# Attention and feed-forward in one planned kernel: products of probabilities and values share the score tiles' PSUM and are tied to a score pair

## The chip, the cores and the metric

The kernel runs on one core of a Trainium2 chip. The metric is the device time of one launch in microseconds (us). A measurement of this kernel can tell two versions apart from about 0.3% on.

## The reference

Block-sparse attention over 4 batches, 8 heads, 768 positions and 64 values per head, and then a feed-forward layer over the 3072 rows that it gives:

```
scores = scale * np.matmul(q, k.transpose(0, 1, 3, 2))
...
scores = np.where(mask, scores, -1000000000.0)
scores = scores - np.max(scores, axis=-1, keepdims=True)
attn = np.exp(scores)
attn = attn / (np.sum(attn, axis=-1, keepdims=True) + 1e-09)
return np.matmul(attn, v).astype(np.float32)
...
x = np.ascontiguousarray(attn_out.transpose(0, 2, 1, 3)).reshape(B * S, H * D)
h = x @ w_in
g = np.maximum(h, 0.0) + alpha * np.minimum(h, 0.0)
return (g @ w_out).astype(np.float32)
```

The mask lets each block of 32 positions see its neighbours, the first and last block and three drawn ones. Here `w_in` is 512x2048 and `w_out` 2048x512.

## The kernel before

**The work.** Everything is cut into chunks of 256 query rows (two tiles of 128), 12 chunks in all. A chunk has 4 units, one for each pair of heads; a unit `u` has two score pairs, one for each head. 32-bit values are split into a high and a low 16-bit part, so each product is taken three times (high by high, high by low, low by high).

**A score pair** is one step of the plan (`emit_s`, L603 to L619). It fills two PSUM tiles `sp` of 128x768 for two row tiles. Its first four matmuls (L611) use TensorE's whole 128x128 array. Its last four (L617) use halves of 64 rows, two matmuls at a time. VectorE then reads each tile (`emit_bias`, L627: scale, mask, row minimum `nm`), which I call the bias below. ScalarE takes the exponential (`emit_exp`, L634). The reciprocal of the row sum (`dn`, `rs`) and the split into `ph` high (`times`, L390 to L394) and low (`rest`, L398 to L401) follow on the engines that the plan chose, and a DMA transposes `ph` into `pt`.

**The products of a unit** (`emit_av`, L664 to L680) multiply `pt` by the split values: 36 matmuls that use halves of 64 columns, two heads side by side. The result `av` (128x256) goes to `x`: ScalarE writes the high part (`emit_x_hi`, L685), then VectorE the low part (`emit_x_lo`, L690). In the kernel before, `av` is a tile of the same pool as the score tiles, which has two buffers (`ps_s`, tag `s`). A score pair needs both.

**The feed-forward work** of a chunk is 8 groups `h` (`emit_up`, 24 matmuls, L1052) and 8 groups `o` (`emit_down`, 12 matmuls, L1094), which run between the pairs of the next chunk. VectorE makes `g` from `h` (L1062, L1063), ScalarE and GpSimd split it into `gh` and `gl`.

**The start.** For the first 125 us or so the kernel also turns the 64-bit weights into 32-bit ones and splits them (`wi`, `wo`; L858 to L870 on VectorE, L863 on ScalarE, L390 to L394, L955 and L960), and finds scales (`gsc`, `am1`).

**What sets the order.** `Plan.run` is a list scheduler that runs while the program is built. Each operation has a priority, the engines that it may run on with an assumed cost for each, the operations that it needs, and the buffers that it takes and frees. The order in which the scheduler starts the operations is the order in which their instructions are written, and each engine carries its own out in that order. The semaphores are put in afterwards by the framework, from the tiles that the written instructions read and write; the scheduler doesn't see them.

Of the kernel before, what the change touches and what calls it, by code (L numbers as in the profile page):

```python
# [8 lines left out]
F32 = mybir.dt.float32  # L9
# [18 lines left out]
MOE_LAG = 10.973  # L28
EARLY = 15.72
MOE_BOOST = 1.244  # L30
V_WA = -11.421
W_WA = 0.818
V_WB = 2.562
W_WB = 0.788
LDP = 47.514
PL_V = -45.149
P_V = 2.094
# [10 lines left out]
PREF = {"PE": 1.0, "DVE": 1.928, "ACT": 1.347, "POOL": 1.033, "SP": 1.0}  # L48
PREF0 = {"PE": 1.0, "DVE": 2.5, "ACT": 1.0, "POOL": 0.8, "SP": 1.0}
SLOW = 1.12  # L50
UNTIL = 130.0
Q_PE = 1
# [8 lines left out]
class Op:  # L61
    def __init__(self, n, prio, alts, fn, deps, alloc, use, dma):
        self.n, self.prio, self.alts, self.fn, self.dma = n, prio, alts, fn, dma
        self.deps = [d for d in deps if d is not None]
        self.alloc, self.use = alloc, use
        self.start = self.done = None
        self.eng = None


class Plan:  # L70
# [14 lines left out]
    def op(self, prio, alts, fn, deps=(), alloc=(), use=(), dma=None):  # L85
        o = Op(len(self.ops), prio, alts, fn, deps, list(alloc), list(use), dma)
        for b in o.alloc + o.use:
            b.users.append(o)
        self.ops.append(o)
        return o  # L90
# [12 lines left out]
    def run(self):  # L103
# [19 lines left out]
        busy = dict.fromkeys(self.ENGINES, 0.0)  # L123

# [28 lines left out]
        while left:  # L153
            progress = True
            while progress:
                progress = False
                ready.sort(key=lambda o: (o.prio, o.n))
                load = dict.fromkeys(self.ENGINES, 0.0)
                taken = []
                for o in ready:  # L160
# [60 lines left out]
def attn_moe(ctx: ExitStack, tc: tile.TileContext, q, k, v, sampled, w_in, w_out, alpha, out):  # L221
# [19 lines left out]
    plan = Plan(dict(bufs, s=2, h=2, o=2, ld=LD))  # L241
# [108 lines left out]
    def mask_cols_pe():  # L350
        mk["c"] = ps_s.tile([P, S], F32, tag="s", name="mk")
# [3 lines left out]
    def mask_rows_pe(t):  # L355
        mk[t] = ps_s.tile([P, S], F32, tag="s", name="mkr")
# [7 lines left out]
    mb = plan.buf("s")  # L364
# [3 lines left out]
    for t in range(NT):  # L368
        mb = plan.buf("s")
# [231 lines left out]
    def emit_s(n):  # L601
# [6 lines left out]
        for i in range(2):  # L608
            T["sp", n + i] = ps_s.tile([P, S], F32, tag="s", name="sp")
# [54 lines left out]
    def emit_av(u):  # L664
# [4 lines left out]
        av = T["av", u] = ps_s.tile([P, S], F32, tag="s", name="av")  # L669
# [109 lines left out]
    def attend(n):  # L779
# [23 lines left out]
    def values(u):  # L803
# [3 lines left out]
        ab = plan.buf("s")  # L807
        if hp == 0:
# [435 lines left out]
```

## Time and profile before

| | |
|---|---|
| Median of 3 runs | 834.72 us (833.66 to 836.19) |
| The profiled execution | 835.07 us, span 833.4 us |
| TensorE (PE) busy | 786.3 us, 94% of the span |
| VectorE (DVE) busy | 664.8 us, 80% |
| ScalarE (ACT) busy | 483.9 us, 58% |
| GpSimd (POOL) busy | 576.0 us, 69% |
| DMA queue q1 | 72.0% of 16 engines' span |

The busy share of TensorE is a mean over two stages: a start of some 126 us in which it has gaps, and the rest, in which it hardly stops. Which of the two a change touches decides what it is worth. A stretch of work that the profile gives as the time from one start to the next is what TensorE really spends on it; the single matmuls' own durations overlap.

### The profile page before, as it was taken

How to read it: one execution, taken by the hardware profiler on the slowest of the kernel's cores; microseconds unless marked ns; L12 is line 12 of the kernel's file. 1: busy time of each engine (PE TensorE's matmuls, PEld its weight loads, DVE VectorE, ACT ScalarE, POOL GpSimd, SP SyncE). 2: the span in 40 equal slices, each digit the busy share in tenths (PEclk: the TensorE clock that was granted, in tenths of full speed). 3: DMA queues.
4: the chain of work that ended last, by engine and by line, in shares of the span. 5: the costliest groups of instructions: out<-in, count | busy, mean ns of one | idle time of the engine just before them, and what ended most of it. 6: DMA issues, size and time to landing. Idle time of an engine off the chain costs nothing. (4 is left out here: it accounts for less than half of the span.)

```text
span 833.4 us, 16815 instructions
## 1 busy us (share of the span) xinstructions
PE 786.3 (94%) x6303; PEld 497.7 (60%) x6303; DVE 664.8 (80%) x1336; ACT 483.9 (58%) x898; POOL 576.0 (69%) x460
## 2 busy tenths in 40 slices
PE   4868669999999999999999999999999999999997
PEld 2423336666666666566665666666666675566764
DVE  5999889879789978788889797888799797676222
ACT  6988966765646455565566373756565564563111
POOL 5398777768768768578758777677878686666221
PEclk9799879999999999999999999999999999999999
DMA  9999784876878776878978758869898565754200
GB/s 336 322 288 227 180 180 98 189 165 148 192 164 193 147 171 116 206 118 200 199 165 174 152 122 169 192 141 203 168 196 147 135 150 117 156 111 107 59 7 25
DMA packets 386449, 136.13 MB, mean 163 GB/s; under 512 B 350628, under 2 KB 379328, under 8 KB 386368
## 3 DMA queue, kind: packets, MB, share of 16 engines
q1 hardware_dynamic: 386304, 135.04, 72.0%
q8 instruction: 49, 0.80, 0.4%
q14 instruction: 32, 0.26, 0.1%
q0 software_dynamic: 64, 0.02, 0.0%
HBM read 35.67 MB, written 6.29 MB: 50 GB/s over the span
## 5 line engine op out<-in xcount | busy, mean ns | idle before, releaser
L1052 PE MATMUL h<-x,wi 128*128 128x256 f16 x2304 | 267.9, 274 | 0.0
L634 ACT ACTIVATE e<-e,nm 128x768 f32<-128x768 f32 x192 | 178.7, 931 | 144.9 <-DVE nm L627 137.0
L1052 PEld LDWEIGHTS <-wi 128*128 128x128 f16 x2304 | 221.0, 98 | 49.3 <-issue 17.3
L1094 PE MATMUL o<-wo,gh 128*128 128x512 f16 x768 | 229.1, 380 | 0.0
L627 DVE CUSTOM_DVE_ANT_0 e<-sp,bias,cs 128x768 f32<-128x768 f32 x192 | 188.8, 1009 | 41.8 <-PE sp L617 41.3
L394 POOL TENSOR_SCALAR ph<-e,rs 128x768 f16<-128x768 f32 x95 | 97.9, 1031 | 144.5 <-PE sp L617 33.5
L401 POOL TENSOR_TENSOR ph<-e,ph 128x768 f16<-128x768 f32 x100 | 188.2, 1882 | 8.3
L1073 POOL TENSOR_TENSOR gl<-g,gh 128x512 f16<-128x512 f32 x96 | 125.3, 1307 | 57.4 <-ACT gh L1068 36.7
L1094 PE MATMUL o<-wo,gl 128*128 128x512 f16 x384 | 145.6, 379 | 0.6 <-POOL gl L1073 0.6
L398 DVE SCALAR_TENSOR_TENSOR ph<-e,rs,ph 128x768 f16<-128x768 f32 x92 | 135.6, 1474 | 4.3 <-ACT ph L390 2.8
L1068 ACT CAST gh<-g 128x512 f16<-128x512 f32 x96 | 59.2, 616 | 127.5 <-DVE g L1063 122.7
L1094 PEld LDWEIGHTS <-gh 128*128 128x128 f16 x768 | 68.8, 98 | 86.7 <-issue 12.8
L400 POOL TENSOR_SCALAR e<-e,rs 128x768 f32<-128x768 f32 x100 | 112.2, 1122 | 10.7 <-ACT ph L390 7.8
L674 PE MATMUL av<-pt,v 128*64 128x256 f16 x1728 | 105.4, 277 | 5.4 <-DVE nm L627 5.2
L1062 DVE SCALAR_TENSOR_TENSOR g<-h,am 128x512 f32<-128x512 f32 x96 | 65.7, 684 | 52.2 <-PE h L1052 52.0
L674 PEld LDWEIGHTS <-v 128*64 128x64 f16 x1728 | 92.1, 111 | 22.4 <-issue 15.2
L390 ACT ACTIVATE ph<-e,rs 128x768 f16<-128x768 f32 x75 | 69.4, 930 | 22.7 <-DVE rs L645 18.7
L1063 DVE SCALAR_TENSOR_TENSOR g<-h,gsc,g 128x512 f32<-128x512 f32 x96 | 72.1, 751 | 3.4
L1094 PEld LDWEIGHTS <-gl 128*128 128x128 f16 x384 | 37.5, 98 | 46.3 <-POOL gl L1073 1.1
L611 PEld LDWEIGHTS <-qt 128*128 128x128 f16 x384 | 37.6, 99 | 35.3 <-issue 13.2
L611 PE MATMUL sp<-kt,qt 128*128 128x512 f16 x192 | 48.2, 334 | 5.8 <-DVE x L690 4.1
L611 PE MATMUL sp<-ks,qt 128*128 128x512 f16 x192 | 48.3, 334 | 1.3 <-DVE nm L627 1.3
(147 smaller groups left out, 763.0 us busy)
## 6 DMA issues: line engine op xcount, KB each, us to landing
wo<-in_moe_w_in_dram SPq DMA_DIRECT2D x16, 512.0 KB, 6.3
raw<-in_moe_w_out_dram SPq DMA_DIRECT2D x16, 512.0 KB, 8.6
kf<-in_k_dram SPq DMA_DIRECT2D x16, 384.0 KB, 3.9
qf<-in_q_dram SPq DMA_DIRECT2D x12, 512.0 KB, 4.9
vf<-in_v_dram SPq DMA_DIRECT2D x16, 384.0 KB, 5.1
out_dram<-ob SPq DMA_DIRECT2D x24, 256.0 KB, 2.5
ks<-kt SPq DMA_DIRECT2D x30, 192.0 KB, 4.3
pt<-ph SPq DMA_TRANSPOSE x192, 3.4
```

Source lines behind the costliest of these rows:

```text
L394: nc.gpsimd.tensor_scalar(dst, src, scale, 1.0, ALU.mult, ALU.mult)
L398: nc.vector.scalar_tensor_tensor(dst, src, scale, hi, ALU.mult, ALU.subtract)
L400: nc.gpsimd.tensor_scalar(tmp, src, scale, 1.0, ALU.mult, ALU.mult)
L401: nc.gpsimd.tensor_tensor(dst, tmp, hi, ALU.subtract)
L611: nc.tensor.matmul(T["sp", n + i][:, a:z], T["qt", u][:, h, i, :], (ks, kt)[i][:, h, a:z], start=True, stop=False)
L627: nc.vector.tensor_tensor_reduce(T["e", n], T["sp", n], bias[:, t0 + j % w, :], scale=T["cs", c][:, hp : hp + 1], scalar=3.0e38, op0=ALU.a ...
L634: nc.scalar.activation(T["e", n], T["e", n], AF.Exp, bias=T["nm", n], scale=-1.0, accum_out=T["su", n])
L674: nc.tensor.matmul(av[h * D : (h + 1) * D, : n * P], v2[:, h, t, vv, :], T["pt", u, h][:, pl * NT + t, :], start=(m == 0), stop=(m == len( ...
L1052: nc.tensor.matmul(ph[:, i, :], win(w, f, ct), x[:, ct, :], start=(m == 0), stop=(m == len(terms) - 1))
L1063: nc.vector.scalar_tensor_tensor(g, ph, gs_[:, j : j + 1], g, ALU.mult, ALU.add)
L1073: nc.gpsimd.tensor_tensor(T["gl", c, j], T["g", c, j], T["gh", c, j], ALU.subtract)
L1094: nc.tensor.matmul(T["o", c][t], g[:, i, t * P : (t + 1) * P], wout(w, f), start=(i == 0 and m == 0 and j in first_j), stop=(i == 1 and m ...
```

## The change

The two score tiles become two fixed tiles of 128x1024, `sp[0]` and `sp[1]`. A score pair uses columns 0 to 767 of both, which its matmuls write in two parts, 0 to 511 and 512 to 767. The products of unit `u` go to columns 768 to 1023 of `sp[u % 2]`, right behind the second part. In the plan the products no longer take a score buffer (`s0` and `s1` are the pair's alone); they need `x` of unit `u - 2` to be done. Each TensorE operation has a mode, the array's division that it starts and ends with: 0 is the whole array, 1 halves of rows, 2 halves of columns. A change of division costs the plan `SWITCH` = 0.095, and while the array stands at 1, products are preferred by `JOIN` = 5.497. The products' own priority is later by `P_AV` = 6.123. Fifteen other numbers of the plan move a little, and the pair's and the products' own assumed costs.

```diff
-MOE_LAG = 10.973
+MOE_LAG = 10.963
...
-P_V = 2.094
+P_V = 2.751
...
+SWITCH = 0.095
+JOIN = 5.497
+P_AV = 6.123
...
-            return s * (sum(c) if isinstance(c, tuple) else c)
+            c = s * (sum(c) if isinstance(c, tuple) else c)
+            return c + SWITCH if e == "PE" and o.mode[0] != tiling else c
...
-                ready.sort(key=lambda o: (o.prio, o.n))
+                ready.sort(key=lambda o: (o.prio - JOIN if o.mode[0] == 2 and tiling == 1 else o.prio, o.n))
...
-    ps_s = ctx.enter_context(tc.tile_pool(name="ps_s", bufs=2, space=PSUM))
+    ps_s = ctx.enter_context(tc.tile_pool(name="ps_s", bufs=1, space=PSUM))
...
+    sp = [ps_s.tile([P, 1024], F32, tag=f"s{i}", name=f"sp{i}") for i in range(2)]
...
-            T["sp", n + i] = ps_s.tile([P, S], F32, tag="s", name="sp")
+            T["sp", n + i] = sp[i][:, :S]
...
-        av = T["av", u] = ps_s.tile([P, S], F32, tag="s", name="av")
+        av = T["av", u] = sp[u % 2][:, S:]
...
-            sbuf[n], sbuf[n + 1] = plan.buf("s"), plan.buf("s")
-            o_s[n] = o_s[n + 1] = plan.op(n, {"PE": 1.17}, lambda: emit_s(n), [o_qt[u], o_av.get(steps[max(n - 3, 0)][0] - 2)] + o_kt[b, hp] + o_ks[b, hp],
-                                          [sbuf[n], sbuf[n + 1]], [qtbuf[u], kbuf[b, hp], ksbuf[b, hp]])
+            sbuf[n], sbuf[n + 1] = plan.buf("s0"), plan.buf("s1")
+            o_s[n] = o_s[n + 1] = plan.op(n, {"PE": 1.07}, lambda: emit_s(n), [o_qt[u], o_av.get(steps[max(n - 3, 0)][0] - 2)] + o_kt[b, hp] + o_ks[b, hp],
+                                          [sbuf[n], sbuf[n + 1]], [qtbuf[u], kbuf[b, hp], ksbuf[b, hp]], mode=(0, 1))
...
-        o = o_av[u] = plan.op(p - 2, {"PE": 0.3 + 1.88 * f}, lambda: emit_av(u), last + [o_v2[b, hp]],
-                    [ab, xbuf[c]], [ptbuf[u, 0], ptbuf[u, 1], vbuf[b, hp]])
+        o = o_av[u] = plan.op(p - 2 + P_AV, {"PE": 0.05 + 1.92 * f}, lambda: emit_av(u), last + [o_v2[b, hp], o_x.get(u - 2)],
+                    [xbuf[c]], [ptbuf[u, 0], ptbuf[u, 1], vbuf[b, hp]], mode=(2, 2))
```

Eight lines are added ahead of the functions in question, so their lines move on by 9: the pair's are L620 and L626 after, the bias L636, the products L683, the high and low part of `x` L694 and L699, `h` L1060 and `o` L1102.

Three places of the two programs follow, with what each instruction waits for. A wait names the engine whose count it waits for; `DMAHW` are DMA transposes and loads.

First TensorE at the products of unit 28, the first of chunk 7. Before:

```order
L617 MATMUL sp_6974<-ks_5911,qt_6511 128x256
L1094 LDWEIGHTS gh_6916 [waits Activation_49]
...
L674 LDWEIGHTS v2_5207 [waits DMAHW1_49,DMAHW0_49]
L674 MATMUL av_7020<-pt_6776,v2_5207 64x256 [waits DVE_49]
...
L1052 LDWEIGHTS wi_88
...
L611 LDWEIGHTS qt_6511
L611 MATMUL sp_7107<-ks_5911,qt_6511 128x512 [waits DVE_49]
```

and after:

```order
L626 MATMUL sp1_74<-ks_5696,qt_6323 128x256
L683 LDWEIGHTS v2_5057 [waits DMAHW1_49]
L683 MATMUL sp0_73<-pt_6521,v2_5057 64x256 [waits DMAHW0_49]
...
L1102 LDWEIGHTS gh_6693 [waits Activation_49]
...
L620 LDWEIGHTS qt_6323
L620 MATMUL sp0_73<-ks_5696,qt_6323 128x512 [waits DVE_49]
```

Before, a group `o` stands between the pair and the products, and a group `h` between the products and the next pair; after, the products stand right behind the pair, and one group `o` is all that lies between them and the next pair, which waits for VectorE.

Second, VectorE at the same unit. Before:

```order
L627 ISA e_7008,nm_7009<-sp_6971,bias_110,cs_6117 128x768 [waits PE_49,Pool_49]
L398 SCALAR_TENSOR_TENSOR ph_7006<-e_6925,rs_6983,ph_7006 128x768 [waits DMAHW5_49,Pool_49]
L627 ISA e_7057,nm_7058<-sp_6974,bias_110,cs_6117 128x768 [waits PE_49]
...
L455 SCALAR_TENSOR_TENSOR qn_6810<-qf_6706,sq_6782,qn_6810 128x8x64
L690 SCALAR_TENSOR_TENSOR x_7019<-av_7020,x_7019 128x256 [waits Activation_49]
```

and after:

```order
L1071 SCALAR_TENSOR_TENSOR g_6754<-h_6706,gsc_121,g_6754 128x512 [waits DVE_49]
L636 ISA e_6798,nm_6799<-sp0_73,bias_112,cs_5854 128x768 [waits PE_49,Pool_49]
L407 SCALAR_TENSOR_TENSOR ph_6757<-e_6697,rs_6752,ph_6757 128x768 [waits DMAHW3_49,Pool_49]
L636 ISA e_6818,nm_6819<-sp1_74,bias_112,cs_5854 128x768
L699 SCALAR_TENSOR_TENSOR x_6759<-sp0_73,x_6759 128x256 [waits Activation_49]
```

The first bias waits for TensorE in both. Before, the count that it waits for is the one that the pair's last matmul on that tile sets; after, it is the one that the last of the 36 matmuls of the products sets, because both touch `sp0`. Of the 192 biases 173 wait for the pair and none for products before; after, 113 wait for the pair and 31 for products. The next pair's first matmul waits for the last row shown (`x`) in both programs.

Third, VectorE at the products of unit 23, the last of chunk 5. Before:

```order
L627 ISA e_5829,nm_5830<-sp_5731,bias_110,cs_4992 128x768 [waits DVE_49]
L627 ISA e_5834,nm_5835<-sp_5734,bias_110,cs_4992 128x768
...
L392 TENSOR_SCALAR ph_5905<-e_5834,rs_5898 128x768 [waits DMAHW6_49,DVE_49]
L690 SCALAR_TENSOR_TENSOR x_5118<-av_5839,x_5118 128x256 [waits Activation_49]
L398 SCALAR_TENSOR_TENSOR v2_5900<-vf_4637,sv_4918,v2_5900 128x12x64 [waits Pool_49]
```

and after, where the products lie in the second tile of the pair:

```order
L636 ISA e_5657,nm_5658<-sp0_73,bias_112,cs_4731 128x768 [waits DVE_49]
L636 ISA e_5701,nm_5702<-sp1_74,bias_112,cs_4731 128x768 [waits PE_49]
L407 SCALAR_TENSOR_TENSOR kn_5655<-kf_5566,ks_5648,kn_5655 128x12x64 [waits DMAHW3_49,DMAHW5_49,DMAHW2_49,Pool_49]
L650 TENSOR_SCALAR dn_5736<-su_5704 128x1 [waits Activation_49]
L654 RECIPROCAL rs_5741<-dn_5736 128x1 [waits DVE_49]
L407 SCALAR_TENSOR_TENSOR v2_5734<-vf_4390,sv_4904,v2_5734 128x12x64 [waits Pool_49]
L699 SCALAR_TENSOR_TENSOR x_4998<-sp1_74,x_4998 128x256 [waits Activation_49]
```

Before, neither bias waits for products, and `x` comes ahead of the values' split. After, the second bias waits for the products' last matmul; the splits of keys (`kn`) and values (`v2`) for the next batch and the low part of `x` stand behind it, and the pair after one group `h` waits for that `x`.

More of the change, by code (lines that the diff above doesn't have):

```diff
@@ L27 @@
 SIZES0 = [2, 2, 2]
-MOE_LAG = 10.973
+MOE_LAG = 10.963
 EARLY = 15.72
[L30 to L36, printed above, removed]
-P_V = 2.094
+MOE_BOOST = 1.237
+V_WA = -11.367
+W_WA = 0.771
+V_WB = 1.288
+W_WB = 0.74
+LDP = 49.245
+PL_V = -45.648
+P_V = 2.751
 PL = "gv"
@@ L47 @@
 LEADL = 2
-PREF = {"PE": 1.0, "DVE": 1.928, "ACT": 1.347, "POOL": 1.033, "SP": 1.0}
-PREF0 = {"PE": 1.0, "DVE": 2.5, "ACT": 1.0, "POOL": 0.8, "SP": 1.0}
+PREF = {"PE": 1.0, "DVE": 1.944, "ACT": 1.355, "POOL": 1.016, "SP": 1.0}
+PREF0 = {"PE": 1.0, "DVE": 2.183, "ACT": 0.98, "POOL": 0.948, "SP": 1.0}
 SLOW = 1.12
 UNTIL = 130.0
+SWITCH = 0.095
+JOIN = 5.497
+P_AV = 6.123
 Q_PE = 1
@@ L83, in buf, with op @@
         return Buf(pools)
-    def op(self, prio, alts, fn, deps=(), alloc=(), use=(), dma=None):
-        o = Op(len(self.ops), prio, alts, fn, deps, list(alloc), list(use), dma)
+    def op(self, prio, alts, fn, deps=(), alloc=(), use=(), dma=None, mode=(0, 0)):
+        o = Op(len(self.ops), prio, alts, fn, deps, list(alloc), list(use), dma, mode)
         for b in o.alloc + o.use:
@@ L123, in run @@
         busy = dict.fromkeys(self.ENGINES, 0.0)
+        tiling = 0
         def finish(o):
@@ L175, in run @@
                             port["from"], port["to"] = now + self.SLACK[best] * o.alts[best][0], now + c
+                    if best == "PE":
+                        tiling = o.mode[1]
                     o.eng, o.start = best, now
@@ L350, in mask_cols_pe @@
     def mask_cols_pe():
-        mk["c"] = ps_s.tile([P, S], F32, tag="s", name="mk")
+        mk["c"] = sp[1][:, :S]
         for a, z in ((0, 512), (512, S)):
@@ L355, in mask_rows_pe @@
     def mask_rows_pe(t):
-        mk[t] = ps_s.tile([P, S], F32, tag="s", name="mkr")
+        mk[t] = sp[t % 2][:, :S]
         for a, z in ((0, 512), (512, S)):
@@ L363, in attn_moe @@
     o_tab.deps.append(plan.op(-20, {"POOL": 9.0}, lambda: None))
-    mb = plan.buf("s")
+    mb = plan.buf("s1")
     o_mc = plan.op(-20, {"PE": 0.9}, mask_cols_pe, [o_tab], [mb], [pbuf])
@@ L368, in attn_moe @@
     for t in range(NT):
-        mb = plan.buf("s")
+        mb = plan.buf(f"s{t % 2}")
         o = plan.op(-12 + 5 * t, {"PE": 0.9}, lambda t=t: mask_rows_pe(t), [o_tc], [mb], [pbuf, pbuf2])
@@ L806, in values @@
         f = w / 2
-        ab = plan.buf("s")
         if hp == 0:
@@ L811, in values @@
         last = [x for n in range(first[u], first[u + 1]) for x in o_pt[n]]
-        o = o_av[u] = plan.op(p - 2, {"PE": 0.3 + 1.88 * f}, lambda: emit_av(u), last + [o_v2[b, hp]],
-                    [ab, xbuf[c]], [ptbuf[u, 0], ptbuf[u, 1], vbuf[b, hp]])
-        o = plan.op(p - 4, {"ACT": 0.1 + 0.2 * f}, lambda: emit_x_hi(u), [o], [], [ab, xbuf[c]])
-        o_x[u] = plan.op(p - 4, {"DVE": 0.1 + 0.25 * f}, lambda: emit_x_lo(u), [o], [], [ab, xbuf[c]])
+        o = o_av[u] = plan.op(p - 2 + P_AV, {"PE": 0.05 + 1.92 * f}, lambda: emit_av(u), last + [o_v2[b, hp], o_x.get(u - 2)],
+                    [xbuf[c]], [ptbuf[u, 0], ptbuf[u, 1], vbuf[b, hp]], mode=(2, 2))
+        o = plan.op(p - 4, {"ACT": 0.1 + 0.2 * f}, lambda: emit_x_hi(u), [o], [], [xbuf[c]])
+        o_x[u] = plan.op(p - 4, {"DVE": 0.1 + 0.25 * f}, lambda: emit_x_lo(u), [o], [], [xbuf[c]])
     al = cpool.tile([P, NF], F32, name="al")
```

6 lines of the change are left out of this document (3 added, 3 removed).

## The prediction

> **What bounds the kernel now.** I read the page's busy shares and slices first, then the busy time of each engine by stretches, the chain that ended last, and the list of who waited for whom.
>
> ```profile
> span 833.4 us, 16815 instructions
> PE 786.3 (94%) x6303; PEld 497.7 (60%) x6303; DVE 664.8 (80%) x1336; ACT 483.9 (58%) x898; POOL 576.0 (69%) x460
> PE   4868669999999999999999999999999999999997
> PEclk9799879999999999999999999999999999999999
> ```
>
> ```profile
> 20.00:126.00 106.00, 76.28 (x522) 39.04 (x522) 97.36 (x223) 90.21 (x142) 76.11 (x62) 0.85 0.96 240
> 200.00:300.00 100.00, 99.74 (x816) 64.41 (x814) 85.07 (x165) 54.42 (x108) 74.06 (x57) 1.00 0.81 174
> 400.00:500.00 100.00, 99.73 (x821) 64.66 (x820) 86.35 (x170) 56.65 (x111) 75.49 (x59) 1.00 0.75 160
> ```
>
> There are two stages. Up to 126 us VectorE is the busy one (third figure, 97.36 of 106 us) and TensorE has gaps. From then on TensorE works 99.7 of every 100 us at full clock, VectorE 85. So in the second stage any TensorE time that falls away is won in full, and any new TensorE wait is lost in full; VectorE has 15 us in 100 to give. What TensorE spends on each group is in the chain (start, time to the next piece, work):
>
> ```profile
> 692.05 2.62 PE h L1052 x24
> 694.67 2.09 PE av L674 x36
> 696.76 2.70 PE o L1094 x12
> 699.45 0.65 PE sp L611 x4
> 700.10 0.43 PE sp L617 x4
> 704.31 2.73 PE h L1052 x24
> 769.18 2.59 PE o L1094 x12
> ```
>
> A group `h` takes 2.62 us behind `o` and 2.73 behind the pair's halved matmuls (L617); a group `o` takes 2.59 behind `h` and 2.70 behind products. So a change of the array's division costs 0.11 us, in both kinds. Who waits:
>
> ```profile
> PE av L674 <- DVE nm L627: 5.2, 2, 4.5
> PE sp L611 <- DVE x L690: 4.1, 4, 2.6
> DVE e L627 <- PE sp L617: 40.9, 28, 2.9
> ```
>
> TensorE's waits at the touched work are few and mostly in the start. VectorE, on the other hand, comes to a bias too early 28 times and waits 1.5 us on average for the pair. These are the places where holding the bias longer bites at once.
>
> **The change, part by part.**
>
> *Fewer changes of division.* In the order, 34 of the 48 product groups stand right behind a pair after the change, none before. Rows to columns is then one change where there were two (back to whole, and on to columns). 34 x 0.11 = 3.7 us less, 32 of the 34 in the second stage where nothing hides it. No row shows a change straight from halved rows to halved columns. Bounds: 0 saved if it costs as much as two, 7.5 if it costs nothing; I take one change, as both kinds in the rows cost the same. By the Trainium skill (TensorEngine Tiling (Array Packing), Key Properties) a switch of the tiling mode drains TensorE, while moving to another tile of the same mode doesn't; by that rule the direct switch is one drain, and this term stays; no run here shows it yet.
>
> *The bias waits for the products.* This is the price. Products and scores lie in one tile, and after the change 31 biases are held until the last of the 36 matmuls is done, 2.09 us later than the pair. VectorE works in order, so everything behind the bias is held too, and the next pair needs both biases and the low part of `x`. Whether TensorE feels it is a comparison of two sums, between the products' end and the next TensorE instruction that waits for VectorE: TensorE's groups against VectorE's rows. The timeline (start, duration, engine) gives VectorE's steps and the gaps between the engines:
>
> ```profile
> 506.71 0.41 DVE L690 SCALAR_TENSOR_TENSOR x<-av,x 128x256 f16<-128x256 f32 x1
> 507.17 0.48 PE L611 MATMUL sp<-kt,qt 128*128 128x512 f16 x2 [0.50 <-DVE x L690]
> 508.48 1.01 DVE L627 CUSTOM_DVE_ANT_0 e<-sp,bias,cs 128x768 f32<-128x768 f32 x1
> 509.41 1.01 DVE L627 CUSTOM_DVE_ANT_0 e<-sp,bias,cs 128x768 f32<-128x768 f32 x1
> 510.35 0.08 DVE L627 DVE_READ_ACCUMULATOR2_ANT nm<- 128x1 f32 x1
> 519.20 0.60 PE L1094 MATMUL o<-wo,gh 128*128 128x512 f16 x2
> 519.41 1.02 DVE L627 CUSTOM_DVE_ANT_0 e<-sp,bias,cs 128x768 f32<-128x768 f32 x1 [2.64 <-PE sp L617]
> ```
>
> and the groups of 200 to 700 us (count, busy us, mean ns) the other durations:
>
> ```profile
> L398 DVE SCALAR_TENSOR_TENSOR ph<-e,rs,ph 128x768 f16<-128x768 f32 x66 | 102.2, 1549 | 1.5 <-ACT ph L390 1.4
> L392 DVE TENSOR_SCALAR ph<-e,rs 128x768 f16<-128x768 f32 x20 | 19.9, 997 | 0.7
> L455 DVE SCALAR_TENSOR_TENSOR qn<-qf,sq,qn 128x512 f16<-128x512 f32 x16 | 17.7, 1108 | 0.0
> L398 DVE SCALAR_TENSOR_TENSOR v<-vf,sv,v 128x768 f16<-128x768 f32 x11 | 14.8, 1347 | 3.3 <-ACT v L390 2.4 <-POOL v L394 0.8
> L398 DVE SCALAR_TENSOR_TENSOR kn<-kf,ks,kn 128x768 f16<-128x768 f32 x9 | 10.6, 1176 | 0.0
> ```
>
> One bias to what follows takes 0.94 us (508.48 to 509.41 to 510.35), some 0.07 less than its own duration, since the next one starts before it has ended; I take the same 0.07 off the other means, and 0.08 for `dn` or `rs`. From the start of TensorE's next group to a bias held by TensorE are 0.21 us (519.20 to 519.41), from the end of `x` to the pair 0.05 (506.71 + 0.41 to 507.17).
>
> - Unit 28, shown in the change, and units 24, 36 and 40 with the same rows: 0.21 + bias 0.94 + low `ph` 1.48 + bias 0.94 + `x` 0.41 + 0.05 = 4.03 us on VectorE, against one group `o` of 2.70: short by 1.3, four times, 5.3 us.
> - Units 23 and 35: 0.21 + bias 0.94 + `kn` 1.11 + `dn`, `rs` 0.16 + `v` 1.28 + `x` 0.41 + 0.05 = 4.16, against `h` 2.73 and half of the pair's first part 0.33: short by 1.1, twice, 2.2 us.
> - Unit 12: 0.21 + bias 0.94 + `rs` 0.08 + `qn` 1.04 + bias 0.94 + `dn` 0.08 + high `ph` 0.93 + `x` 0.41 + 0.05 = 4.68, against `h` 2.73: short by 1.9.
> - Units 4, 6, 8 and 11, summed in the same way over stretches of 3 to 15 us, are short by 1.4, 0.6, 1.0 and 0.3: 3.3 us.
>
> Together 12.7 us. The same comparison over the order of before finds no stretch that is short, and indeed its TensorE hardly waits there. Below: 0, if VectorE is late at these biases anyway. Above: with the full durations instead of the steps, and 1.09 for a bias with its read-out, the same sum is 31 us after and 9 before, so 22 more. I take 12.7, since the smaller steps are the ones that fit the 99.7 of 100.
>
> The Trainium skill has the rule that speaks against the change (PSUM — Partial Sum Buffer, PSUM bank collisions raise a hardware error): two engines must not touch one bank (512 of these columns) and 32-partition quadrant at once, even at other columns of it, so their accesses have to be put in order. Score columns 512 to 767 and the products at 768 to 1023 are one bank by that. By this rule the held bias is no accident of this order, and 845 us stands; without it the scores could be read while the products run, which would give 831. Before, products and scores had tiles of their own, so its trace can't show this.
>
> *The score buffers.* Products take no score tile any more. That ends the wait of 4.5 us and its like, which lie in the start, where VectorE is what the end hangs on. In the second stage a pair still waits for `x` of the last products on its tile.
>
> *The start.* TensorE has the same number of instructions ahead of its first group `h` in both programs, and the same work behind it. VectorE gets more to do ahead of the scale `gsc`: two L865, one high part of `wi` and four of `wo`, one copy of `qt`, one `rs`, and five `dn` fewer.
>
> First the pair and the first `h` of before, then those groups up to 126 us:
>
> ```profile
> 125.49 0.55 PE L611 MATMUL sp<-kt,qt 128*128 128x512 f16 x2 [2.61 <-DVE x L690]
> 126.72 0.61 PE L1052 MATMUL h<-x,wi 128*128 128x256 f16 x2
> ```
>
> ```profile
> L865 DVE SCALAR_TENSOR_TENSOR wo<-raw,wo 128x512 int32<-128x512 int32 x3 | 2.7, 898 | 0.1
> L392 DVE TENSOR_SCALAR wi<-wi,ssc 128x512 f16<-128x512 f32 x2 | 1.5, 762 | 0.0
> L641 DVE TENSOR_SCALAR dn<-su 128x1 f32<-128x1 f32 x14 | 2.0, 143 | 1.8 <-ACT e L634 1.8
> L556 ACT COPY qt<-qp 128x512 f16<-128x512 f16 x4 | 2.6, 700 | 0.0
> ```
>
> 2 x 0.90 + 5 x 0.76 + 0.70 (the copy by ScalarE's row, VectorE has none) + 0.15 - 5 x 0.14 = 5.8 us. VectorE was idle for 106 - 97.4 = 8.6 us there, and ScalarE gets less to do. Bounds: -4 (the buffer waits were on the path) to +5.8 (nothing absorbs it). I take +1.5, between them and nearer to a busy VectorE.
>
> *Covered.* The other numbers of the plan only move work about; the tile's address itself costs nothing, as the matmuls' shapes stay.
>
> **The sum.** The profiled execution took 835.07 us, 0.35 above the median of the runs. 835.1 - 3.7 + 12.7 + 1.5 = 845.6; less 0.35, about 845.
>
> **Rivals.**
>
> 1. *VectorE has room, faster.* If VectorE comes to the held biases later than the products end, because ScalarE or GpSimd hold it ahead of them, term two is 0 and 835.1 - 3.7 = 831. For it: VectorE has 15 us in 100 free, and two rows of `g` stand ahead of the bias at unit 28. Against it: the 40.9 us that it waits for pairs already. It decides as soon as TensorE's new waits stay under 3.7 us together, that is under 0.35 at each of the eleven places. Chance 0.18.
> 2. *It cancels.* If VectorE is half late at the held biases, the places are short by some 4 us together; with no change in the start 835.1 - 3.7 + 4 - 0.35 = 835. Chance 0.09.
> 3. *No change of division is saved*, since rows to columns passes through the whole array: 845 + 3.7 = 849. Against it: nothing in the rows needs it. Chance 0.13.
> 4. *The start is late by all of the 5.8 us*, and delayed biases reach ScalarE's and GpSimd's parts too: 850 or more. Chance 0.13.
>
> **How the numbers follow.** The forecast (840 to 848) has 0.47, and 845 is its middle. 0.3%, 2.5 us, is about what a measurement of this kernel can tell from no change. Slower by more: 0.47 + 0.13 + 0.13 = 0.73; within: 0.09; faster: 0.18. The range goes from 832, which leaves out about half of rival 1, to 857, which leaves out the end of rival 4 and with it the 22 us. Among the slower cases alone it is 840 to 857.
>
> **What would show it.** In the profile after: chain rows in which `h` or `o` behind a pair's products and nothing else is 0.11 longer, and products right behind a pair still at 2.09 (one change; 2.20 for rival 3). A wait of the bias for products (L636 <- PE, L683) of many us on VectorE. TensorE waits of 1 to 2 us on `x` (L699) and on `nm` (L636) at units 12, 23, 24, 28, 35, 36 and 40, some 13 us in all after the first `h`; busy TensorE in 200 to 700 us down from 99.7 to about 98. The first `h`, at 126.7 before, between 124 and 132 us. The prediction is wrong if VectorE waits for products but TensorE doesn't wait for VectorE.

## The result: 846.7 us, 1.45% slower, and the profile after

| | before | after |
|---|---|---|
| Median, 4 runs each on one chip | 834.83 us (833.66 to 836.19) | 846.74 us (846.01 to 848.27) |
| Ratio, 95% interval | | 1.0145 (1.0123 to 1.0166) |
| The profiled execution, its span | 835.07 us, 833.4 us | 848.27 us, 846.1 us |
| First `h` after the span's start | 126.7 us | 132.3 us |
| TensorE idle behind it, gaps over 0.1 us | 2.8 us in 7 | 13.1 us in 20 |

The forecast was 845. From the page of the changed kernel:

```profile
span 846.1 us, 16778 instructions
PE 787.1 (93%) x6303; PEld 501.7 (59%) x6303; DVE 649.7 (77%) x1345; ACT 474.8 (56%) x885; POOL 565.3 (67%) x463
```

TensorE has the same busy time in a longer span, and VectorE less. The busy time by stretches shows where the slack went (TensorE is the second figure, VectorE the fourth):

```profile
20.00:126.00 106.00, 75.39 (x488) 38.08 (x486) 96.06 (x201) 81.13 (x129) 68.29 (x54) 0.87 0.86 224
200.00:300.00 100.00, 98.77 (x828) 64.33 (x828) 79.95 (x167) 58.48 (x113) 76.34 (x60) 1.00 0.91 179
400.00:500.00 100.00, 98.35 (x811) 64.65 (x809) 81.85 (x166) 51.75 (x104) 70.30 (x57) 1.00 0.77 161
```

TensorE fell from 99.7 to 98.4 and 98.8 of 100, and VectorE is idle for longer. Who waits for whom from 160 us on, behind the start (TensorE to 800 us, VectorE to 760; us in total, times, longest):

```profile
PE sp L620 <- DVE x L699: 7.5, 10, 1.8
...
DVE e L636 <- PE sp L683: 30.6, 24, 3.2
DVE e L636 <- PE sp L626: 2.2, 4, 0.7
```

The bias hardly waits for the pair any more (L626, 2.2 us, where it was 40.9 before) but for the products (L683, 30.6 us), and the next pair waits for the `x` that stands behind those biases. At unit 28, the place that the prediction worked through, the timeline shows it link by link (start, duration):

```profile
500.80 0.27 PE L626 MATMUL sp<-ks,qt 64*128 64x256 f16 x1
501.00 2.16 PE L683 MATMUL sp<-pt,v 128*64 128x256 f16 x36
503.08 0.60 PE L1102 MATMUL o<-wo,gh 128*128 128x512 f16 x2
503.33 1.02 DVE L636 CUSTOM_DVE_ANT_0 e<-sp,bias,cs 128x768 f32<-128x768 f32 x1 [1.43 <-PE sp L683]
504.27 1.26 DVE L407 SCALAR_TENSOR_TENSOR ph<-e,rs,ph 128x768 f16<-128x768 f32 x1
505.45 1.00 DVE L636 CUSTOM_DVE_ANT_0 e<-sp,bias,cs 128x768 f32<-128x768 f32 x1
506.39 0.41 DVE L699 SCALAR_TENSOR_TENSOR x<-sp,x 128x256 f16<-128x256 f32 x1
506.85 0.48 PE L620 MATMUL sp<-ks,qt 128*128 128x512 f16 x2 [1.00 <-DVE x L699]
```

The pair is complete by 501.1, yet the bias starts at 503.33, 0.25 behind the start of the group that follows the products. From 503.08 to the next pair VectorE needs 3.77 us, one group `o` lasts 2.77, and TensorE idles for 1.00. The first two rows show the other side: from the pair's last matmul to the products are 0.20 us, against 0.11 for a step without a change (the 24 matmuls of an `h` in 2.62 us), and the products take 2.08 from start to start. So rows to columns is one change of about 0.09, not two. The Trainium skill's rule on mode switches (TensorEngine Tiling (Array Packing), Key Properties), by which TensorE drains at each switch, fits that.

The start came out later than forecast. VectorE's scale `gsc` is ready 10.8 us later, at 133.52 instead of 122.73 (the first row is before, the second after):

```profile
122.73 0.17 DVE L924 TENSOR_TENSOR gsc<-rg,ro 128x8 f32<-128x8 f32 x1
```

```profile
133.52 0.17 DVE L932 TENSOR_TENSOR gsc<-rg,ro 128x8 f32<-128x8 f32 x1
```

and TensorE, which begins `h` at 132.33, then stops again and again in the first 25 us of the second stage:

```profile
132.33 0.50 PE L1060 MATMUL h<-x,wi 128*128 128x256 f16 x3
134.29 4.64 PE L1060 MATMUL h<-x,wi 128*128 128x256 f16 x41 [0.68 <-DVE x L699]
139.79 0.48 PE L620 MATMUL sp<-kt,qt 128*128 128x512 f16 x2 [0.54 <-DVE nm L636]
144.05 2.79 PE L1060 MATMUL h<-x,wi 128*128 128x256 f16 x24 [1.25 <-DVE g L1071]
157.50 0.48 PE L620 MATMUL sp<-kt,qt 128*128 128x512 f16 x2 [0.85 <-DVE nm L636]
```

The balance of the two profiled executions: first `h` +5.6, TensorE's gaps behind it +10.3, everything else behind it -3.2 (702.7 - 2.8 = 699.9 before, 709.8 - 13.1 = 696.7 after). That makes 12.7, the difference of the spans. Ahead of the first `h` both programs have the same 576 matmuls, so the three parts can be compared. The -3.2 is not the saving of divisions alone. The first 48 matmuls `h` took 6.60 us before, at a mean granted clock of 0.81, and 5.74 without the waits between them after, at 1.00; that makes 0.9 of it. A stop also costs more than its gap: the matmuls just ahead of the stops took 1.1 us longer than in an unbroken row before, over 7 stops, and 3.0 us after, over 20. So the saving is better read from the single steps, as the third experiment does.

### The profile page after: what moved, and what is told of

It is laid out like the page before. It is cut to its first block, busy times and chain, and to the rows that moved or that the text cites. A ratio compares the mean times of both kernels' runs of the same rounds, so it can differ in the third digit from the quotient of the medians.

```text
span 846.1 us, 16778 instructions
## 1 busy us (share of the span) xinstructions
PE 787.1 (93%) x6303; PEld 501.7 (59%) x6303; DVE 649.7 (77%) x1345; ACT 474.8 (56%) x885; POOL 565.3 (67%) x463
## 4 chain that ended last, share of the span: by engine, by line
PE 74%; DVE 15%; ACT 5%; issue 4%; DMA 1%; POOL 1%; POOLq 0%; SPq 0%; DVEq 0%; ACTq 0%
PE o L1102 25%; PE h L1060 24%; PE sp L683 11%; PE sp L620 6%; DVE e L636 4%; PE sp L626 4%; DVE ph L407 2%; ACT e L643 2%; PE d L963 1%; DVE wo L407 1%; DVE qn L464 1%; DMA wo<-in_moe_w_in_dram 1%; DVE x L699 1%; DVE wo L866 1%; DVE v L407 1%
## 5 line engine op out<-in xcount | busy, mean ns | idle before, releaser
L1060 PE MATMUL h<-x,wi 128*128 128x256 f16 x2304 | 267.7, 273 | 2.1 <-DVE g L1071 1.3
L1060 PEld LDWEIGHTS <-wi 128*128 128x128 f16 x2304 | 222.7, 98 | 49.0 <-issue 8.0
L1102 PE MATMUL o<-wo,gh 128*128 128x512 f16 x768 | 229.0, 380 | 0.0
L636 DVE CUSTOM_DVE_ANT_0 e<-sp,bias,cs 128x768 f32<-128x768 f32 x192 | 190.1, 1009 | 40.9 <-PE sp L683 34.0
L1081 POOL TENSOR_TENSOR gl<-g,gh 128x512 f16<-128x512 f32 x96 | 122.6, 1278 | 110.2 <-ACT gh L1076 89.9
L410 POOL TENSOR_TENSOR ph<-e,ph 128x768 f16<-128x768 f32 x100 | 176.4, 1764 | 8.4
L403 POOL TENSOR_SCALAR ph<-e,rs 128x768 f16<-128x768 f32 x90 | 99.9, 1111 | 74.0 <-DVE rs L654 17.5
L1102 PE MATMUL o<-wo,gl 128*128 128x512 f16 x384 | 145.5, 379 | 0.6 <-POOL gl L1081 0.6
L407 DVE SCALAR_TENSOR_TENSOR ph<-e,rs,ph 128x768 f16<-128x768 f32 x92 | 121.3, 1319 | 6.8 <-ACT ph L399 3.4
L1102 PEld LDWEIGHTS <-gh 128*128 128x128 f16 x768 | 69.8, 98 | 85.7 <-issue 14.7
L409 POOL TENSOR_SCALAR e<-e,rs 128x768 f32<-128x768 f32 x100 | 106.8, 1068 | 12.3 <-ACT ph L399 5.4
L683 PE MATMUL sp<-pt,v 128*64 128x256 f16 x1728 | 107.6, 281 | 3.5 <-DVE nm L636 3.4
L683 PEld LDWEIGHTS <-v 128*64 128x64 f16 x1728 | 94.2, 113 | 19.5 <-issue 18.6
L399 ACT ACTIVATE ph<-e,rs 128x768 f16<-128x768 f32 x80 | 74.2, 928 | 15.6 <-DVE rs L654 8.5
L620 PEld LDWEIGHTS <-qt 128*128 128x128 f16 x384 | 37.1, 99 | 51.8 <-issue 33.7
L1102 PEld LDWEIGHTS <-gl 128*128 128x128 f16 x384 | 37.5, 98 | 46.3 <-POOL gl L1081 1.1
L620 PE MATMUL sp<-ks,qt 128*128 128x512 f16 x192 | 48.1, 333 | 8.9 <-DVE x L699 6.4
L620 PE MATMUL sp<-kt,qt 128*128 128x512 f16 x192 | 47.9, 331 | 5.1 <-DVE nm L636 3.6
```

Source lines behind the costliest of these rows:

```text
L399: nc.scalar.activation(dst, src, AF.Copy, scale=scale)
L403: nc.gpsimd.tensor_scalar(dst, src, scale, 1.0, ALU.mult, ALU.mult)
L407: nc.vector.scalar_tensor_tensor(dst, src, scale, hi, ALU.mult, ALU.subtract)
L409: nc.gpsimd.tensor_scalar(tmp, src, scale, 1.0, ALU.mult, ALU.mult)
L410: nc.gpsimd.tensor_tensor(dst, tmp, hi, ALU.subtract)
L620: nc.tensor.matmul(T["sp", n + i][:, a:z], T["qt", u][:, h, i, :], (ks, kt)[i][:, h, a:z], start=True, stop=False)
```

## The experiments

Theory A is that of the prediction: biases held by products make TensorE wait. Theory B, its rival, is that the changed order and its numbers cost the time, wherever the products lie. C and D are two readings of the later start. Each kernel was timed in five rounds, and taken against the kernel before on the same chip. "Idle" is TensorE's gaps behind the first `h`.

| run | median us | ratio (95%) | first `h` | idle |
|---|---|---|---|---|
| e1 second tile | 840.3 | 1.0061 (1.0049 to 1.0074) | 130.1 | 8.6 |
| e2 first tile | 853.1 | 1.0223 (1.0207 to 1.0240) | 137.4 | 14.8 |
| e3 whole array between | 849.1 | 1.0173 (1.0159 to 1.0187) | 131.4 | 12.7 |
| e4 start's numbers | 844.8 | 1.0120 (1.0106 to 1.0133) | 128.6 | 12.0 |
| e5 not joined | 844.8 | 1.0119 (1.0103 to 1.0135) | 130.0 | 8.8 |
| e6 plan knows | 835.4 | 1.0008 (0.9998 to 1.0018) | 132.5 | 2.4 |
| e7 = e6 + e1 | 843.2 | 1.0102 (1.0088 to 1.0116) | 136.9 | 4.4 |
| e8 = e4 + e1 | 839.3 | 1.0057 (1.0043 to 1.0070) | 126.1 | 6.8 |
| e9 = e8, plan knows from 130 | 833.2 | 0.9985 (0.9976 to 0.9994) | 125.6 | 3.5 |
| e10 = e9, second tile in the start alone | 833.4 | 0.9990 (0.9981 to 0.9999) | 126.3 | 4.2 |
| e11 = e4, plan knows from 130 | 834.2 | 0.9998 (0.9989 to 1.0006) | 127.0 | 4.2 |
| e12 = after, plan knows from 130 | 840.7 | 1.0071 (1.0059 to 1.0083) | 129.9 | 7.7 |

### Which tile holds the products (e1, e2)

```diff
-        av = T["av", u] = sp[u % 2][:, S:]
+        av = T["av", u] = sp[1][:, S:]      # e2: sp[0]
```

> The changed kernel, with the products of every unit behind the second score tile instead of behind the two in turn. The order of the work, the number of changes of division and the start stay. A pair's first bias reads the first tile, so it can run beside the products, and only the second bias has to wait for them. Theory A (a bias that must wait for products on its tile is what TensorE's new waits of 10.3 us behind the first h come from): the hold of the first bias goes from about 2.1 us to the 1.1 us that VectorE needs for it anyway; by the same two-engine sum as in the prediction the shortfall goes from 12.7 to 3.4 us, so about 837.5 us, 9 less than the changed kernel, 0.3% above the kernel before. Theory B (the new waits come from the changed order of the work, whatever tile holds the products): TensorE's idle time behind the first h stays near 13 us, the time stays at 846 to 847.

> The changed kernel, with the products of every unit behind the first score tile. Order, divisions and start stay. Every first bias that stands behind products is now held by them, and the second with it. Theory A (the held bias costs TensorE its waits): the shortfall by the two-engine sum is 14.1 us against 12.7 of the changed kernel, so 847 to 850 us, and VectorE's wait of the bias for products rises from 31.8 us. Theory B (the order alone): 846 to 847 with that wait anywhere.

VectorE's list of waits in e1, from 160 us on, and unit 28 on the timeline:

```profile
DVE e L636 <- PE sp L683: 12.4, 13, 1.6
DVE e L636 <- PE sp L626: 6.3, 12, 1.0
```

```profile
497.55 2.16 PE L683 MATMUL sp<-pt,v 128*64 128x256 f16 x36
498.03 1.01 DVE L636 CUSTOM_DVE_ANT_0 e<-sp,bias,cs 128x768 f32<-128x768 f32 x1
499.64 0.61 PE L1102 MATMUL o<-wo,gh 128*128 128x512 f16 x2
499.93 1.00 DVE L636 CUSTOM_DVE_ANT_0 e<-sp,bias,cs 128x768 f32<-128x768 f32 x1
```

The first bias now runs while the products do (498.03 lies inside 497.55 to 499.64), and only the second is held. In the traces of e1 and e2 the order of the instructions on TensorE, VectorE, ScalarE and GpSimd is the changed kernel's from the first to the last, and yet e1 is 6.4 us faster. The pair e4 and e8, which differ by the same edit, have one order as well and are 5.4 us apart. TensorE's gaps at units 12, 24, 28, 36 and 40 (1.11, 0.91, 1.00, 1.76 and 0.94 us after the change, 5.7 together) are gone. All five are even units, whose products lay behind the first tile. At units 23 and 35, whose products lay behind the second tile already, the gaps stay, 0.51 and 0.52. At unit 20, where the products wait for a running bias of their tile, the gap grew from 0.30 to 1.24. So theory B falls for these five places. The gain was less than the 9 expected; the gaps of the first 30 us stay.

e2 lost 6.4 where 0 to 3 were expected, and VectorE's wait of the bias for products did not rise (31.9 us from 130 us on, 31.8 in the changed kernel). Its gaps grew by 1.7; most of the rest is the start, where the first `h` came 5.1 us later. There the wait also goes the other way, from a bias to the products on its tile:

```profile
131.09 0.99 DVE L636 CUSTOM_DVE_ANT_0 e<-sp,bias,cs 128x768 f32<-128x768 f32 x1
132.15 4.05 PE L683 MATMUL sp<-pt,v 128*64 128x256 f16 x36 [1.97 <-DVE nm L636]
137.43 1.75 PE L1060 MATMUL h<-x,wi 128*128 128x256 f16 x12
```

Part of it is the clock: these products took 4.05 us instead of 2.16, and TensorE's granted clock was 0.50 from 132 to 136 us.

### The change of division (e3)

```diff
+        nc.tensor.matmul(av[:, 0:1], ident16, nident[:, 0:1], start=True, stop=True)
```

> The changed kernel, with one matmul of the whole array and a single column ahead of every unit's products, written into the place that the products then overwrite (48 small matmuls more). It undoes the change of division: every products' group is now reached through the whole array, as before the change. Theory A (a change of division costs about 0.09 us each, and rows to columns costs one change, not two): 34 changes more, 34 x 0.09 = 3.1 us, and 48 matmuls of some 0.03 to 0.06 us, 1.4 to 2.9 us: 850 to 853 us, and the step from the small matmul to the products is 0.09 above a plain step while the step from the pair to the small matmul is longer by as much. Theory B (rows to columns costs as much as two changes, and the 3.1 us behind the first h have another cause): only the 1.4 to 2.9 us of the small matmuls, 847 to 849 us.

TensorE at unit 28 in e3:

```profile
502.10 0.27 PE L626 MATMUL sp<-ks,qt 64*128 64x256 f16 x1
502.30 0.18 PE L680 MATMUL sp<-nident,ident 128*128 128x1 f16 x1
502.40 2.16 PE L684 MATMUL sp<-pt,v 128*64 128x256 f16 x36
504.49 0.61 PE L1103 MATMUL o<-wo,gh 128*128 128x512 f16 x2
```

From the pair to the small matmul are 0.20 us, the same step as straight to the products, and 0.10 to 0.11 more to the products. Little of that is the small matmul itself: where it stands behind an `h`, the way to the products is 0.109 + 0.107 us in the trace, against 0.202 without it. So the detour costs a change of division of 0.10 and 0.01 for the matmul. The 32 such places behind the first `h` make 32 x 0.11 = 3.5 us, the other small matmuls 0.2. That is what the time behind the first `h` shows without its gaps (713.2 - 12.7 = 700.5, against 696.7). In the medians 2.4 arrive; in this profile the first `h` came 0.9 us earlier. The total, 849.1, lies at the upper end of theory B's 847 to 849 and below theory A's 850 to 853, which had put the small matmuls at 1.4 to 2.9 us. The steps decide for theory A: the saving of the change is real, and a direct change costs as much as one.

### The start's numbers (e4, e8)

```diff
-V_WA, W_WA, V_WB, W_WB, LDP, PL_V, P_V = -11.367, 0.771, 1.288, 0.74, 49.245, -45.648, 2.751
+V_WA, W_WA, V_WB, W_WB, LDP, PL_V, P_V = -11.421, 0.818, 2.562, 0.788, 47.514, -45.149, 2.094
-PREF0 = {"PE": 1.0, "DVE": 2.183, "ACT": 0.98, "POOL": 0.948, "SP": 1.0}
+PREF0 = {"PE": 1.0, "DVE": 2.5, "ACT": 1.0, "POOL": 0.8, "SP": 1.0}
```

The seven single lines of the first row are written as one here.

> The changed kernel, with the eight numbers of the plan that place the loads, weights and q, k, v of the start as the kernel before has them; the tiles, the joining to a pair and all other numbers stay as changed. VectorE then has 104.7 us of work ahead of the scale of the expert weights instead of 110.7 (105.8 in the kernel before), by the same durations. Theory C (the 5.6 us by which the first h comes later are VectorE's extra weight work ahead of that scale): the first h comes at 125 to 128 us again, and the two-engine shortfall behind it is 13.3 against 12.7, so about 841 to 842 us. Theory D (the later start comes from the shared tiles, by biases that wait for products in the start): the first h stays at 131 to 133 us and the time at 846 to 847.

> The two single edits together: the products of every unit behind the second score tile, and the eight numbers of the start from the kernel before. The second tile alone gave 840.3, the start alone 844.8, against 846.7. If the parts are separate (one takes the held first bias away in the second stage, the other VectorE's weight work ahead of the scale): 838.4 us, first h at 126 to 128 us. If both act on the same thing in the start (biases held there): 840 us, as the second tile alone, since its first h came at 130.1 already.

In e4 the first `h` came 3.8 us earlier, at 128.6, between what theories C and D expected, but the time fell by only 2.0. Other numbers make another order in the second stage too, and its held biases cost as much as before (idle 12.0, by other places). In e8 the first `h` is back at 126.1. Its 839.3 lies between the two expectations, 838.4 and 840, so it does not tell them apart. What the start is worth came out only once the holds were planned for, below.

### Products not tied to the pair (e5)

```diff
-JOIN = 5.497
-P_AV = 6.123
+JOIN = 0.0
+P_AV = 0.0
```

> The changed kernel with the two numbers that tie a unit's products to a score pair (JOIN and P_AV) at zero; the shared tiles and all other numbers stay. 11 products' groups then stand right behind a pair instead of 34, and of the biases behind products 11 wait for them instead of 31. Theory A (holds cost): the two-engine shortfall goes from 12.7 to 4.3 us, of which the first changed run showed four fifths, so 6 to 7 us less idle time of TensorE behind the first h; 23 changes of division come back, 23 x 0.11 = 2.5 us. 842 to 844 us. Theory B (the order and its other numbers cost, not the holds): 849 us, the changes of division on top of the changed kernel's time.

844.8, just above what theory A expected and 4 below theory B. VectorE's waits for products fell from 30.6 us to 6.3 and TensorE's gaps by 4.3, of 6 to 7 expected; some 2 us of division changes came back. The two medians, 1.9 us apart, are within 0.3% of each other, and the first `h` came 2.3 us earlier in e5. Behind it e5's profile is 3.0 us shorter (706.8 to the end of TensorE's work, against 709.8). So with a plan that doesn't know the hold, tying the products to a pair costs at least what it saves.

### A plan that knows the hold (e6, e7)

```diff
+                    if o.mode == (0, 1) and any(x is not None and x.done is None for x in behind):
+                        continue
+                    if o.mode[0] == 2 and any(k.start is not None and k.done is None for k in o.readers):
+                        continue
...
+                    if o.mode[0] == 2:
+                        behind[o.tile] = o.low
+                        for k in o.readers:
+                            if k.start is None and all(d.start is not None for d in k.deps if d.mode == (0, 1)):
+                                need[k.n] += 1
+                                kids[o.n].append(k)
+                                held.append(k)
```

`readers` are the biases of the products' tile, `low` is its low part of `x`; biases in `held` wait for the products in the plan as they do on the chip. e7 adds the edit of e1.

> The changed kernel, its tiles in turn as changed, but its plan made to know the hold: in the planner, products that start make the biases of their tile wait that haven't started, products wait for a bias of their tile that runs, and the next pair waits for the transposed low part that shares the tile. Nothing else is edited; the order changes at many places. By the sums 13 biases wait for products, 30 products' groups stand right behind a pair, the two-engine shortfall is 0.2 us, and VectorE has 107.6 us ahead of the scale of the expert weights (changed kernel 110.7, before 105.8). Theory A (holds that the plan doesn't see cost the idle time): behind the first h TensorE idles 3 to 5 us and the time is 834 to 839 us. Theory B (a hold costs the same wherever it is put, or other waits come in its place): 843 us or more.

> The planner that knows the hold, with the products of every unit behind the second score tile. By the sums 11 biases wait for products, 38 products' groups stand right behind a pair (four more than in the changed kernel), the two-engine shortfall is 0, and VectorE has 105.1 us ahead of the scale, 0.7 less than in the kernel before. Theory A: the first h at 126 to 129 us, TensorE idle 3 to 4 us behind it, 38 x 0.09 = 3.5 us saved by divisions: 831 to 835 us, the kernel before or a little less. Theory B (the order costs, or the hold wherever it stands): 838 us or more.

e6 took 835.4, as theory A expected: 11.3 us less than the changed kernel, with the same shared tiles and 30 products still right behind a pair. Its waits from 160 us on:

```profile
PE sp L638 <- DVE nm L654: 0.5, 1, 0.5
...
DVE e L654 <- PE sp L644: 13.8, 14, 2.4
DVE e L654 <- PE sp L701: 3.2, 6, 0.8
```

Biases wait for products 3.2 us (L701) instead of 30.6, and TensorE's gaps are down to 2.4 us, below the kernel before. The hold is the same; it has been put where VectorE had nothing to do or something else to do. e7 missed by 8 us, and its 843.2 is in the range of its theory B. Behind the first `h` it is nearly as good as e6 (idle 4.4), but its start, in an order of its own, put the first `h` at 136.9 instead of 126 to 129. The simple reading of theory C falls here, that the first `h` hangs on the work ahead of `gsc` alone. In e6 the scale is ready 7.7 us earlier than in the changed kernel, and the first `h` comes no earlier:

```profile
125.80 0.17 DVE L955 TENSOR_TENSOR gsc<-rg,ro 128x8 f32<-128x8 f32 x1
```

```profile
132.46 3.04 PE L1083 MATMUL h<-x,wi 128*128 128x256 f16 x24
```

TensorE's granted clock from 120 to 130 us was 0.50 in e6 and 0.83 in the changed kernel, so a slower TensorE is a rival for this that no run tells apart.

### Knowing it only behind the start (e9 to e12)

```diff
-                    if o.mode[0] == 2:
+                    if o.mode[0] == 2 and now >= UNTIL:     # the same in the two rules above
```

> The second tile for every unit and the start's eight numbers of before, as in the run of the two together, and the planner knows the hold, but only from its time 130 on, so that the start stays in the order of that run. There its first h came at 126.1 us, as in the kernel before (126.7). By the sums the shortfall behind it is 0 and 32 products' groups stand right behind a pair. If the parts are separate (start: weight work and held biases; second stage: holds against changes of division): first h at 126, some 570 ns x 0 new waits, 32 x 0.097 = 3.1 us saved, so 830 to 832 us, faster than the kernel before by 2 to 4 us. If holds only move (a plan that delays biases leaves VectorE late elsewhere): 836 to 840 us, TensorE idle 6 us or more behind the first h.

> As the run with the second tile for all, but only the four units of the start have their products behind the second tile; from unit 4 on the tiles are in turn. Planner's rules from its time 130 on, the start's numbers of before. By the sums the shortfall behind the first h is 2.1 us in one place, 33 products' groups stand right behind a pair. If the parts are separate: first h at 126, idle some 3 us, 830 to 834 us. If holds only move: 836 to 840 us.

> As the mixed one, but with the tiles in turn from unit 0 on. Order and shortfall are the same, only the products of units 0 and 2 lie behind the first tile. If biases held in the start are a cost of their own: the first h comes 2 to 2.5 us later than in the mixed run, as between the two runs with the start's numbers (128.6 against 126.1), and the time is longer by 1.5 to 2.5 us. If that difference was only the spread from one execution to the next: the same within 0.3%.

> The changed kernel with one thing more: from its time 130 on the planner knows the hold. The start, its numbers and the tiles in turn stay as changed, so everything ahead of the first h is in the changed kernel's order. By the sums the shortfall behind the first h is 2.1 us in one place and 35 products' groups stand right behind a pair. If the start (about 5.6 us to the first h) and the holds behind it are separate terms: the first h at 130 to 133 us, TensorE's idle time behind it down from 13 to 6 or less (some of what stands in the first 30 us behind the first h is VectorE's lateness from the start and stays), 836 to 840 us. If the holds in the second stage were worth less than the sums say, 842 us or more.

e12 has the changed kernel's order, instruction for instruction on all four engines, up to 213 us. It is 6.0 us faster than that kernel, so what the edit wins lies behind 213 us. The time is 0.7 above what was expected, and TensorE idles 7.7 us instead of 6 or less. The stops of the first 25 us are all still there, as the order there is the same:

```profile
131.88 4.64 PE L1083 MATMUL h<-x,wi 128*128 128x256 f16 x41 [0.71 <-DVE x L717]
137.38 0.49 PE L638 MATMUL sp<-kt,qt 128*128 128x512 f16 x2 [0.54 <-DVE nm L654]
141.63 2.79 PE L1083 MATMUL h<-x,wi 128*128 128x256 f16 x24 [1.25 <-DVE g L1094]
155.34 0.48 PE L638 MATMUL sp<-kt,qt 128*128 128x512 f16 x2 [0.85 <-DVE nm L654]
```

They stay in e1 as well, so the tile of the products does not make them. They are gone in e8 and e11, which have the start's numbers of before. So those 4 us go with the order of the start, out of which VectorE comes late. They are gone in e6 too (0.2 us), which has the changed kernel's numbers but an order of its own from about 92 us on; so the numbers alone do not make them either. e11 differs from e12 by these numbers alone (and by what the plan makes of them later) and is 6.5 us faster: 840.7 to 834.2. The two steps, 6.0 for holds and 6.5 for the start, are the whole way from 846.7 back to the time of the kernel before. Taken in the other order, by e4, they are 2.0 for the start and 10.5 for the holds (844.8 to 834.2), since the order that e4's plan makes of the second stage has other held places. What each is worth alone depends on the order that it is put into; that the two together are the loss doesn't. "Start" here means all that these eight numbers move, held biases in the start included.

e9 took 833.2 where 830 to 832 were expected, e10 833.4, within its 830 to 834. e11 was to be 1.5 to 2.5 us longer than e10 if holds in the start cost something of their own, and was 0.84 longer, just about the 0.3% (2.5 us) of "the same"; its first `h` came 0.7 later, with the same order on all four engines. What the second tile does in this start is not told apart from the spread, then. e9 is 0.15% faster than the kernel before, a gain whose interval leaves out 1 only narrowly. Its waits from 160 us on:

```profile
PE sp L638 <- DVE nm L654: 1.9, 2, 1.1
PE sp L638 <- DVE x L717: 0.2, 1, 0.2
...
DVE e L654 <- PE sp L701: 7.4, 8, 1.4
```

This is the fastest of these twelve, and shows what the change has to give: the 3 us of the divisions, less 0.7 of gaps and 0.9 by which its first 48 matmuls `h` were slower than before; 1.1 of its lead in the profile is an earlier first `h`.

## Why the prediction came out right, and where it did not

**The total** is right, 846.7 for 845, and so is the cause that carried the sign. That it came within 2 us is luck: in the changed kernel's own order two terms were wrong by about as much in opposite directions.

**Fewer changes of division**, forecast 3.7 us. A change costs 0.09 to 0.10 us by the steps, not 0.11, so 32 x 0.097 = 3.1 behind the first `h`; e3 gave it back. That a direct change costs one and not two was right, and rival 3 falls with it.

**The bias waits for products**, forecast 12.7. The mechanism is right, and most of the places: TensorE stops at all seven units that the prediction named for the second stage. The rule of the Trainium skill on a bank's quadrants (PSUM — Partial Sum Buffer, PSUM bank collisions raise a hardware error) asks for the order that the rows at unit 28 show, where the bias stood still until the products were done. Whether the hold goes away with a bank of its own for the products was not tried. The size was too big: with the start as it is, a plan that knew the holds won 6.0 (e12). The "some 13 us in all" were met, 13.1, but not by the places: the seven named units hold 6.8, for which the sum had 9.4, and 3.8 stand in the first 30 us. Three things in the sum failed.

- The four places behind an `o` were put at 1.3 each, 5.3 in all, and are 0.91, 1.00, 1.76 and 0.94, 4.6 in all. At unit 28 the low `ph` took 1.18 to the next bias, not the 1.48 from the mean of before; its mean itself fell, as the groups of 134 to 760 us after show:

```profile
L407 DVE SCALAR_TENSOR_TENSOR ph<-e,rs,ph 128x768 f16<-128x768 f32 x84 | 109.0, 1298 | 5.5 <-ACT ph L399 3.2 <-POOL ph L403 2.1
```

Why VectorE does this faster after the change is open.
- Unit 12 was put at 1.9 and units 23 and 35 at 1.1 each. They idle for 1.11, 0.51 and 0.52.
- Of the 3.3 for units 4, 6, 8 and 11, unit 6 shows 0.35, unit 11 0.12 and unit 8 nothing. The stops around unit 4, in the first 30 us, go with the order of the start: e1 has them too, e8, e11 and e6 have not.

**The start**, forecast +1.5 between -4 and +5.8. This step failed: the size was taken from "a busy VectorE" near the middle of its bounds. The first `h` came 5.6 later, at the upper bound (3.2 later in e12, in the same order), and VectorE's lateness went on behind it for 4 us more, which the term did not hold at all. e12 against e11 puts the start at 6.5 in all. The price list was short as well: the four high parts of `wo` took 1.26 us each, not the 0.76 taken from those of `wi`, and the 16 instructions L866 on `wo` (L858 before), whose number did not change, took 11.2 us instead of 8.9; the same step for `wi` took 10.6 instead of 11.7. The list also left out biases held in the start: before, VectorE waited 0.1 us ahead of its 22 biases, after 5.1, and 3.4 of it for products. The rows up to 126 us before and up to 131 us after:

```profile
L858 DVE TENSOR_SCALAR wo<-raw 128x512 int32<-128x512 int32 x16 | 8.9, 567 | 0.0
L627 DVE CUSTOM_DVE_ANT_0 e<-sp,bias,cs 128x768 f32<-128x768 f32 x22 | 21.9, 1005 | 0.1
```

```profile
L866 DVE TENSOR_SCALAR wo<-raw 128x512 int32<-128x512 int32 x16 | 11.2, 714 | 0.0
L401 DVE TENSOR_SCALAR wo<-wo,swo 128x512 f16<-128x512 f32 x4 | 5.0, 1261 | 0.0
L636 DVE CUSTOM_DVE_ANT_0 e<-sp,bias,cs 128x768 f32<-128x768 f32 x22 | 22.0, 1004 | 5.1 <-PE sp L683 3.4 <-PE sp L626 1.7
```

**The rivals.** Rival 1 asked that TensorE's new waits stay under 3.7 us; they were 10.3. Rival 2 had the places at some 4 us and the start unchanged; the named ones alone came to 6.8, and the start moved. Rival 4 was half right, in that the start was late by almost all of its bound, but the total stayed under 850. The first `h` at 132.3 is just outside the 124 to 132 that were named as its sign. What exactly sets the first `h` is open. VectorE's work ahead of `gsc` does not do it alone (e6, e7). The tile moved it by 0.7 us in e11 against e10, which is within the spread, by 2.4 in e8 against e4, and by 5.1 in e2 against the changed kernel, there partly by the clock.

## What to carry to other kernels

When two results share a PSUM tile, price the wait of the reader that comes behind the later writer. At each place, set the time that the reading engine needs from there to the next thing it owes against the other engine's work up to it. If the order comes from a planner, tell it of the wait before turning its numbers: the same shared tiles cost 6 to 10 us with a plan that did not see it and next to nothing with one that did. And when a sum comes out right, test its terms singly: two of these were off by 6.7 and 5 us, one up and one down.

## What the hardware showed that was not expected

The same start does not take the same time. With one order up to the first `h`, it came at 132.33 in the changed kernel and at 129.89 in e12, 2.4 us apart; with another at 126.1, 125.6 and 126.3 (e8 to e10). The spans of the changed kernel's four executions, all in this one order, go from 843.9 to 846.1. So a single profile settles a start only to about 2 us.

The first matmuls `h` do not always run at full clock. In e9 the first 48 took 7.46 us, where the changed kernel needed 0.50 + 0.60 + 4.64 for its 48. The granted clock (the figure third from the end) was 0.66 in these 10 us of e9 and 1.00 from 130 to 140 us in the changed kernel. The first two rows are e9's, the third is the changed kernel's:

```profile
125.63 7.46 PE L1083 MATMUL h<-x,wi 128*128 128x256 f16 x48
```

```profile
120.00:130.00 10.00, 6.49 (x34) 3.49 (x31) 9.82 (x22) 6.52 (x14) 6.46 (x6) 0.66 0.51 116
```

```profile
130.00:140.00 10.00, 7.98 (x71) 5.58 (x66) 8.87 (x25) 6.55 (x14) 6.80 (x7) 1.00 0.61 137
```

How early the first `h` comes does not decide this. In e7, where the first `h` came as late as 136.9, the 48 took 7.58 us, at a granted clock of 0.67 from 130 to 140 us:

```profile
130.00:140.00 10.00, 7.01 (x49) 4.20 (x46) 9.97 (x20) 7.23 (x14) 7.42 (x6) 0.67 0.57 128
```

In e1, with the first `h` at 130.1, they took 5.74 us without the waits between them, at 1.00. What sets the clock at that moment no run here shows. Between e1 and e7 it is worth 1.8 us.
